# A linear-attention and gated-MLP kernel: ScalarE copies transposed bf16 blocks out of PSUM as fp32 words

## The chip, the cores and the metric

The kernel runs on one core of a Trainium2 chip. A core has TensorE (PE; its weight loads are shown as PEld), VectorE (DVE), ScalarE (ACT), GpSimd (POOL), the SyncE queue (SP) that issues most DMAs, an on-chip memory of 128 partitions (SBUF), and a small one of 8 banks (PSUM) that TensorE writes and VectorE and ScalarE read. The metric is the device time of one execution in microseconds (us). Before the change it is 141.28 us, the median of 3 runs (141.26 to 141.32).

## The reference, cut to what matters

The first stage is a gated linear attention over 4 batches x 8 heads, 768 tokens and 48 columns per head; the second takes its output, all heads side by side (384 columns), through a gated MLP that mixes tokens.

```python
for t in range(S):
    state = alpha[:, :, t, :, None] * state + einsum('bhd,bhe->bhde', k[:, :, t], v[:, :, t])
    y[:, :, t] = einsum('bhd,bhde->bhe', q[:, :, t], state)
x = y.transpose(0, 2, 1, 3).reshape(B, S, H * D)

h = maximum(x @ w_in, 0)
u, v = h[..., :512], h[..., 512:]
v_n = (v - mean(v)) / sqrt(var(v) + 1e-6)
v_s = einsum('ts,bsd->btd', w_spatial, v_n) + b_spatial[None, :, None]
out = (u * v_s) @ w_out
```

## The kernel before, in words

The recurrence is done in chunks of 128 tokens, 6 per batch and 24 in all. Within a chunk the cumulative sum of log(alpha) gives the decays, so that a chunk is a masked product of q and k with v, plus q times the state that the chunks before left. The first eight chunks are done as four **pairs** (function `pair`): 256 tokens are loaded with even and odd tokens next to each other in one partition, so that DMA pieces are longer. The other sixteen chunks are **single** (function `first`).

Products need their contracted dimension on the partitions, so four kinds of blocks are transposed by TensorE, as a matmul of the block with a bf16 identity `ident`. Their bf16 results lie in a PSUM bank and are copied to SBUF by ScalarE or VectorE:

- k and q of a pair (transposes at L502, copies in `ev`, tiles `kT` and `qT`, both named kqT): 512 columns a copy;
- k and q of a single chunk (L710, copies in `ev_qk`, tile `kqT`): 64 columns of 8 blocks, 512 a copy, two copies a chunk;
- the attention output x of a chunk (function `finish_x`; first cast to bf16 as `x_sb`): for a pair's chunk three transposes of 128 columns at L365 and one copy `xe` of 384 columns to `xT`, always by ScalarE; for a single chunk six transposes of 64 columns at L389 and two copies of 192;
- the spatial weight (L831, copies in `weights`, tile `w_spT`): two copies of 384 for each of six row blocks.

All these copies go through the helper `copy` (L196 to L200): `nc.scalar.copy` for ScalarE is L198 in the profile, `tensor_copy` for VectorE and GpSimd L200. For a pair, x comes out of the attention with even tokens first and odd tokens after them. The transposes at L365 keep that order, and the copy `xe` restores the order of tokens: it reads its bank at columns 0, 64, 1, 65 and so on and writes in a row.

The second stage's matmuls (v, u, the spatial mix and the output) are all recorded at L819. Elementwise work around them: `relu` to `v_sb` and `uT` (L204 on ScalarE, L206 on VectorE), normalization (L884 to L916, on VectorE `vn` at L916), the masks of the attention scores (`ptm`, L585 for pairs, L756 for single chunks), the decayed q (`qt`, L481 and L691), and the gate (`gT`, L980).

The order of all this is written out by hand. Every step is an `Op` with a number and the engines that it may run on; the string `PLAN` names for each step its engine and place (`P` TensorE, `D` VectorE, `A` ScalarE, `G` GpSimd, `S` the SyncE queue), and `replay` emits the steps in that order. So each engine's order is fixed, and an engine waits at a step until what it needs is there. PSUM banks are handed out in turn, eight in a ring. Numbers behind a colon in the plan are columns of `junk` matmuls (L188) that TensorE runs ahead of a step early in the kernel.

The pair's transposes and copy, which the change edits:

```python
for ks in range(KS):
    nc.tensor.transpose(xv[:, ks, :], st["x_sb"][:, ks, :], ident)
...
copy(eng, bt[b]["xT"][:, c].rearrange("p k (t two) -> p k t two", two=2),
     st["xv"].rearrange("p k (two t) -> p k t two", two=2))
```

Of the kernel before, what the change touches and what calls it, by code (L numbers as in the profile page):

```python
# [9 lines left out]
FP32 = mybir.dt.float32  # L10
# [114 lines left out]
def kernel(  # L125
# [70 lines left out]
    def copy(eng, out, in_):  # L196
        if eng == "ACT":
            nc.scalar.copy(out=out, in_=in_)  # L198
        else:
            ENG[eng].tensor_copy(out=out, in_=in_)  # L200

    def relu(eng, out, in_):
        if eng == "ACT":
            nc.scalar.activation(out=out, in_=in_, func=AF.Relu)  # L204
        else:
            ENG[eng].tensor_scalar_max(out=out, in0=in_, scalar1=0.0)  # L206
# [140 lines left out]
    def finish_x(i):  # L347

        b, c = divmod(i, NCH)
        t0 = c * C  # L350
        st = T[i]
        P = float(10 * i)

        def xs(eng):
            st["x_sb"] = work.tile([128, KS, 128], BF16, name="x_sb")
            copy(eng, st["x_sb"], st["y"].rearrange("p h d -> p (h d)").rearrange("p (k t) -> p k t", k=KS))

        op(("xs", i), {"ACT": 0.38, "DVE": 0.47}, None, xs, got(("y", i), ("xt", i - WK)), prio=P + 9, use=[st["sl_y"]])

        if i // 2 in PAIRS:  # L360
            def xt(_):
                xv = st["xv"] = st["y"].rearrange("p h d -> p (h d)").bitcast(BF16)[:, 0:KS * 128].rearrange(
                    "p (ks t) -> p ks t", ks=KS)
                for ks in range(KS):
                    nc.tensor.transpose(xv[:, ks, :], st["x_sb"][:, ks, :], ident)  # L365

            op(("xt", i), "PE", 0.2, xt, got(("xs", i)), prio=P + 9, use=[st["sl_y"]], cols=384)

            def xe(eng):
                if b not in bt:  # L370
                    tiles(b)
                copy(eng, bt[b]["xT"][:, c].rearrange("p k (t two) -> p k t two", two=2),
                     st["xv"].rearrange("p k (two t) -> p k t two", two=2))

            made[("xe", i)] = [op(("xe", i), ENGINES["xe"], None, xe,
                                  got(("xt", i)) + [made.get(("all", b - 3))], prio=P + 9, use=[st["sl_y"]])]
            return

        sls = [st["sl_y"], Slot(ring)]
        to = {}  # L380

        def xt(_):
            flat = [st["y"].rearrange("p h d -> p (h d)"), bank([128, DM])]
            for r in range(2):
                to[r] = flat[r].bitcast(BF16)[:, 0:KS * 64].rearrange("p (ks t) -> p ks t", ks=KS)
            for ks in range(KS):
                for r in range(2):
                    rows = slice(64 * r, 64 * r + 64)
                    nc.tensor.transpose(to[r][:, ks, :], st["x_sb"][rows, ks, :], ident[rows, rows])  # L389

        op(("xt", i), "PE", 0.1, xt, got(("xs", i)), prio=P + 9, take=sls[1], use=[st["sl_y"]], cols=192)
        made[("xe", i)] = []
        for r in range(2):
            def xe(eng, r=r):
                if b not in bt:
                    tiles(b)
                copy(eng, bt[b]["xT"][:, c, :, 64 * r:64 * r + 64], to[r])

            made[("xe", i)].append(op(
                ("xe", i, r), {"ACT": 0.25, "DVE": 0.22}, None, xe,  # L400
                got(("xt", i)) + [made.get(("all", b - 3))], prio=P + 9, use=[sls[r]]))
# [12 lines left out]
    def pair(j):  # L414
# [33 lines left out]
        for par in range(2):  # L448
            def cum(_, par=par):
                cm = st[f"cum{par}"] = bank([128, 512])  # L450
                for p2 in range(2):
                    nc.tensor.matmul(  # L452
                        out=cm[:, 0:DM], lhsT=lt_pair if p2 > par else le_pair, rhs=lap[:, p2, :, 0:D],
                        start=(p2 == 0), stop=(p2 == 1))

            op(("cump", j, par), "PE", 0.33 + 0.1, cum, got(("lnp", j), ("c_tri",)), prio=P + 2, take=sl_c[par], cols=768)

            def einv(_, par=par):
                st[f"binv{par}"] = binvp_bufs[(2 * j + par) % 3]
                nc.scalar.activation(  # L460
                    out=st[f"binv{par}"], in_=st[f"cum{par}"][:, 0:DM].rearrange("p (h d) -> p h d", h=H),
                    func=AF.Exp, scale=-1.0)

            op(("einvp", j, par), "ACT", 0.38, einv, got(("cump", j, par), ("ktp", *divmod(2 * j + par - 3, 2))), prio=P + 3,
               use=[sl_c[par]])

            def eexp(_, par=par):
                cv = st[f"cum{par}"][:, 0:DM]
                nc.scalar.activation(out=cv, in_=cv, func=AF.Exp)

            op(("eexpp", j, par), "ACT", 0.38, eexp, got(("einvp", j, par)), prio=P + 3.1, use=[sl_c[par]])

            def ktf(eng, par=par):
                ENG[eng].tensor_mul(
                    out=k_blocks(ktp[:, par])[:, :, :, 0:D],
                    in0=quad(st["kc"][:, :, par, :]), in1=quad(st[f"binv{par}"]))

            op(("ktp", j, par), {"POOL": 0.9, "DVE": 0.6}, None, ktf, got(("einvp", j, par), ("kc", 2 * j), ("c_kt", j % NKP)) + tr_users("k", jo), prio=P + 4)

            def qtf(_, par=par):  # L480
                nc.vector.tensor_mul(  # L481
                    out=qtp[:, par, :, ::-1, 0:D], in0=quad(st["qc"][:, :, par, :]),
                    in1=quad(st[f"cum{par}"][:, 0:DM].rearrange("p (h d) -> p h d", h=H)))

            op(("qtp", j, par), "DVE", 0.47, qtf, got(("eexpp", j, par), ("qc", 2 * j), ("c_qt", j % NKP)) + tr_users("q", jo), prio=P + 4, use=[sl_c[par]])

            def vbf(eng, par=par):
                if "vb" not in st:
                    st["vb"] = pairs.tile([128, 2, H, D], BF16, name="vbp", bufs=3)
                copy(eng, st["vb"][:, par], st["vc"][:, :, par, :])  # L490

            op(("vbp", j, par), {"POOL": 0.47, "ACT": 0.42, "DVE": 0.27}, None, vbf, got(("vc", 2 * j), ("y", 2 * j - 5), ("y", 2 * j - 6)), prio=P + 4.5)

            for nm, bufs in (("k", ktp), ("q", qtp)):
                hold = {}
                sl = Slot(ring)

                def tr(_, par=par, nm=nm, bufs=bufs, hold=hold):
                    pt = bank([128, 512])
                    hold["t"] = pt.bitcast(BF16).rearrange("p (n t) -> p n t", n=8)[:, 0:HP, :]  # L500
                    for hp in range(HP):
                        nc.tensor.transpose(  # L502
                            hold["t"][:, hp, :],
                            k_window(bufs[:, par], hp, 1) if nm == "k"
                            else bufs[:, par, hp].rearrange("p s d -> p (s d)"), ident)

                op(("tr", nm, j, par), "PE", 0.22, tr, got((nm + "tp", j, par), ("c_id",)), prio=P + 5, take=sl, cols=512)

                def ev(eng, par=par, nm=nm, hold=hold):
                    if nm == "k":  # L510
                        if "kT" not in st:
                            st["kT"] = work.tile([128, 2, HP, C], BF16, name="kqT", bufs=4)
                        copy(eng, st["kT"][:, par], hold["t"])
                    else:
                        if "qT" not in st:
                            st["qT"] = work.tile([128, 2, HP, C], BF16, name="kqT", bufs=4).rearrange(
                                "p a h c -> p (a h c)").rearrange("p (h c a t) -> p h c a t", a=2, c=2, h=HP)
                        copy(eng, st["qT"][:, :, :, par, :], hold["t"].rearrange("p h (c t) -> p h c t", c=2))

                op(("ev", nm, j, par), EV, None, ev,  # L520
                   got(("tr", nm, j, par), ("y", 2 * j - 4), ("y", 2 * j - 3), ("sc", j - 2, 0), ("sc", j - 2, 1)),
                   prio=P + 6, use=[sl])
# [102 lines left out]
    def first(i):  # L625
# [91 lines left out]
        for r in range(2):  # L717
            def ev_qk(eng, r=r):
                if "kqT" not in st:
                    st["kqT"] = work.tile([128, 2, HP, C], BF16, name="kqT", bufs=4).rearrange("p a h c -> p (a h) c")  # L720
                copy(eng, st["kqT"][:, :, 64 * r:64 * r + 64], hold[r])

            op(("ev", i, r), ENGINES["ev"], None, ev_qk, got(("trk", i), ("y", i - WK), ("sc", i - WK)),
               prio=P + 6, use=[sls[r]])
# [96 lines left out]
    def weights():  # L821
        for tt in range(NT):
# [12 lines left out]
            op(("wt", tt), "PE", 0.2, emit, got(("cast", "w_sp", tt // 2, tt % 2)), prio=50.0, take=sls, cols=384)  # L835
            for r in range(2):
                def ev(eng, tt=tt, hold=hold, r=r):
                    copy(eng, w_spT[:, tt, :, 64 * r:64 * r + 64], hold[r])

                op(("we", tt, r), {"DVE": 0.3, "ACT": 0.42}, None, ev, got(("wt", tt)), prio=50.0, use=[sls[r]])  # L840

# [318 lines left out]
```

## Time and profile before

| What | Value |
|---|---|
| Median time of 3 runs | 141.28 us (141.26 to 141.32) |
| Span of the profiled execution, first to last instruction | 144.3 us (no other time of this execution is given) |
| Busy: PE, DVE, ACT, POOL | 136.8, 118.7, 106.8, 86.8 us |
| Mean granted TensorE clock | 0.996 |
| Copies of transposed blocks by ScalarE | 24 of kqT, 27 of xT, 5 of w_spT |
| Copies of transposed blocks by VectorE | 24 of kqT, 13 of xT, 7 of w_spT |

A row of a group gives line, engine, operation, the tile written and those read (`out<-in`), partitions x elements and type of each, how many; then busy us, mean ns of one, and the idle time of the engine just before them with what ended it. The mean of one is longer than its share of a queue: instructions that follow each other overlap. The chain of waits goes back from the last instruction, at each step to what released it or to the instruction before it on its engine; its pieces are shown in order of time. "issue" is time in which an engine waited for nothing that the profile shows.

### The profile page before, as it was taken

What the parts mean: (1) busy time and instruction counts of PE and PEld (TensorE: products, weight loads), DVE (VectorE), ACT (ScalarE), POOL (GpSimd) and SP (SyncE); (2) the same over time, 40 slices, a digit from 0 to 9 for tenths busy, and PEclk for the clock granted to TensorE, in tenths of its full rate; (3) what the DMA queues carried; (4) which work ended last, traced back from release to release, by engine and by line L of the source; (5) the groups of instructions that cost most, each with busy time, mean ns of one, the idle gap of its engine ahead of it and who ended that gap; (6) DMA issues with size and microseconds to landing.
All of it is one profiled execution on the core that took longest, in us unless ns stands there. A gap on an engine that the chain in (4) does not pass through costs nothing.

```text
span 144.3 us, 4963 instructions
## 1 busy us (share of the span) xinstructions
PE 136.8 (95%) x1915; PEld 84.2 (58%) x1915; DVE 118.7 (82%) x289; ACT 106.8 (74%) x278; POOL 86.8 (60%) x152
## 2 busy tenths in 40 slices
PE   7799999799799999999999999999999999999990
PEld 3334766656465765676556665665657666555560
DVE  7015798899999969899999999999979897987940
ACT  3473479899895879899997789998797698861031
POOL 6856179892709979981249789511599687002820
PEclk9999999999999999999999999999999999999998
DMA  4999999929899989999899899799999241090055
GB/s 108 321 326 351 282 250 325 344 58 259 181 269 191 300 164 182 205 181 214 169 211 222 175 174 185 152 204 196 212 239 227 66 172 55 0 354 28 5 191 191
DMA packets 89000, 28.64 MB, mean 198 GB/s; under 512 B 83728, under 2 KB 87440, under 8 KB 88976
## 3 DMA queue, kind: packets, MB, share of 16 engines
q1 hardware_dynamic: 88944, 28.32, 79.5%
q8 instruction: 15, 0.25, 0.7%
q14 instruction: 9, 0.07, 0.1%
q0 software_dynamic: 32, 0.00, 0.0%
HBM read 23.60 MB, written 4.72 MB: 196 GB/s over the span
## 4 chain that ended last, share of the span: by engine, by line
PE 78%; DVE 8%; ACT 5%; DMA 3%; issue 3%; SPq 0%; ACTq 0%; DVEq 0%
PE bank L819 47%; PE bank L188 4%; DMA ac<-in_alpha_dram 3%; PE bank L710 3%; PE bank L452 2%; PE bank L502 2%; PE bank L745 2%; PE bank L574 2%; DVE ptm L756 2%; PE bank L773 2%; PE bank L731 2%; PE bank L544 1%; DVE ptm L585 1%; PE bank L657 1%; PE bank L601 1%
## 5 line engine op out<-in xcount | busy, mean ns | idle before, releaser
L819 PE MATMUL bank<-w_spT,vn 128*128 128x384 bf16 x192 | 36.3, 326 | 0.1
L980 POOL TENSOR_TENSOR gT<-vsb,uT 128x384 bf16<-128x384 f32 x28 | 25.7, 927 | 11.7 <-DVE vsb L967 11.2
L335 POOL TENSOR_TENSOR state<-state,bc 128x192 f32<-128x192 f32 x20 | 10.3, 513 | 21.4 <-DVE state L328 6.2
L819 PEld LDWEIGHTS <-vn 128*128 128x128 bf16 x192 | 17.1, 97 | 10.2 <-issue 0.2
L756 DVE TENSOR_TENSOR ptm<-bank,mask 128x512 bf16<-128x512 f32 x32 | 20.8, 682 | 1.0 <-ACT xT L198 1.0
L819 PE MATMUL bank<-xT,w_in 128*128 128x384 bf16 x96 | 19.4, 326 | 0.0
L967 DVE TENSOR_TENSOR vsb<-bank,bsp_bc 128x384 f32<-128x384 f32 x31 | 16.7, 554 | 3.2 <-PE bank L819 2.8
L819 PE MATMUL bank<-w_in,xT 128*128 128x512 bf16 x72 | 18.8, 379 | 0.0
L198 ACT COPY kqT<-bank 128x512 bf16<-128x512 bf16 x24 | 13.6, 590 | 6.9 <-PE bank L502 4.4
L819 PE MATMUL bank<-w_out_sb,gT 128*128 128x384 bf16 (+1 forms) x100 | 18.4, 320 | 0.1
L681 POOL TENSOR_TENSOR kt<-kc,binv 128x384 bf16<-128x384 f32 x13 | 12.0, 927 | 6.6 <-ACT bc L676 2.7
L200 POOL CAST sbd<-state 64x192 bf16<-64x192 f32 x40 | 13.6, 341 | 2.1
L884 DVE BATCH_NORM_STATS2 stats<-v_sb 128x6 f32<-128x512 bf16 x20 | 13.6, 681 | 0.5 <-ACT v_sb L204 0.5
L204 ACT ACTIVATE v_sb<-bank 128x512 bf16<-128x512 f32 x20 | 11.9, 608 | 1.6 <-PE bank L819 1.6
L198 ACT CAST x_sb<-bank 128x384 bf16<-128x384 f32 x21 | 10.2, 493 | 3.5 <-PE bank L773 2.7
L819 PEld LDWEIGHTS <-w_in 128*128 128x128 bf16 x96 | 8.7, 97 | 6.0
L188 PE MATMUL bank<-junk 128*128 128x512 f32 (+2 forms) x16 | 11.1, 838 | 1.1 <-DVE halves_of L264 1.1
L200 DVE COPY kqT<-bank 128x512 bf16<-128x512 bf16 x24 | 9.2, 415 | 3.1 <-PE bank L502 2.3
L819 PEld LDWEIGHTS <-gT 128*128 128x128 bf16 x100 | 8.7, 97 | 5.1 <-POOL gT L980 0.2
L204 ACT ACTIVATE uT<-bank 128x384 bf16<-128x384 f32 x23 | 11.3, 495 | 0.3 <-PE bank L819 0.2
L198 ACT COPY xT<-bank 128x192 bf16<-128x192 bf16 (+1 forms) x27 | 9.1, 378 | 2.4 <-PE bank L365 1.5
L585 DVE TENSOR_TENSOR ptm<-bank,mask 128x512 bf16<-128x512 f32 x16 | 10.2, 682 | 0.7 <-PE bank L574 0.4
(128 smaller groups left out, 285.2 us busy)
## 6 DMA issues: line engine op xcount, KB each, us to landing
ac<-in_alpha_dram SPq DMA_DIRECT2D x16, 192.0 KB, 3.9
kc<-in_k_dram SPq DMA_DIRECT2D x16, 192.0 KB, 4.2
qc<-in_q_dram SPq DMA_DIRECT2D x16, 192.0 KB, 4.0
vc<-in_v_dram SPq DMA_DIRECT2D x16, 192.0 KB, 3.8
raw_w<-in_moe_w_spatial_dram SPq DMA_DIRECT2D x3, 768.0 KB, 4.5
out_dram<-raw_w SPq DMA_DIRECT2D x11, 192.0 KB, 2.0
out_dram<-o_sb SPq DMA_DIRECT2D x9, 192.0 KB, 1.9
ac<-in_alpha_dram SPq DMA_DIRECT2D x4, 384.0 KB, 5.5
```

Of the source, the lines that this page charges most:

```text
L188: nc.tensor.matmul(out=flat[:, 0:cols].rearrange("p (a b) -> p a b", a=4), lhsT=junk, rhs=junk[:, None, 0:n].to_broadcast([128, 4, n]), st ...
L198: nc.scalar.copy(out=out, in_=in_)
L200: ENG[eng].tensor_copy(out=out, in_=in_)
L204: nc.scalar.activation(out=out, in_=in_, func=AF.Relu)
L335: ENG[eng].tensor_tensor(out=st["state"], in0=st["state"], in1=st["bc"][:, :, None].to_broadcast([128, HP, D]), op=ALU.mult)
L585: nc.vector.tensor_tensor(out=st[f"ptm{par}"][:, s], in0=st[f"pt{s}{par}"], in1=mask2[:, par], op=ALU.mult)
L681: ENG[eng].tensor_mul(out=k_blocks(kt3)[:, :, :, 0:D], in0=quad(st["kc"]), in1=st["binv"])
L756: nc.vector.tensor_tensor(out=st["ptm"][:, s], in0=st[f"pt{s}"], in1=mask4, op=ALU.mult)
L819: return lambda ps: nc.tensor.matmul(out=out(ps), lhsT=lhsT(), rhs=rhs(), start=start, stop=stop)
L884: nc.vector.bn_stats(out=stats, in_=d["v_sb"][:, tt, :])
L967: nc.vector.tensor_tensor(out=hold["vs"], in0=ps[:, 0:TH], in1=bsp_bc[:, th, :], op=ALU.add)
L980: ENG[eng].tensor_tensor(out=bt[b]["gT"][:, dsl, cols], in0=hold["vs"], in1=bt[b]["uT"][:, dsl, cols], op=ALU.mult)
```

## The change

On ScalarE, the copies of transposed blocks take both sides as fp32, so that two bf16 elements that lie next to each other are moved as one 4-byte word and an instruction has half the elements. On VectorE they stay as they are. For this the two elements of a word must stay neighbours, which the pair's copy of x, with its order of columns, did not allow. So there the transposes themselves now put tokens in order: the identity is read with its columns in the order 0, 64, 1, 65 and so on, and the copy is a plain one. The bank is written in a row as before. The numbers of instructions, their order on each engine and `PLAN` are the same.

```diff
+    def copy_pairs(eng, out, in_):
+
+        copy(eng, *((out.bitcast(FP32), in_.bitcast(FP32)) if eng == "ACT" else (out, in_)))
+
...
                 for ks in range(KS):
-                    nc.tensor.transpose(xv[:, ks, :], st["x_sb"][:, ks, :], ident)
+                    nc.tensor.transpose(
+                        xv[:, ks, :].rearrange("p (t a) -> p t a", a=2), st["x_sb"][:, ks, :],
+                        ident.rearrange("p (a t) -> p t a", a=2))
...
-                copy(eng, bt[b]["xT"][:, c].rearrange("p k (t two) -> p k t two", two=2),
-                     st["xv"].rearrange("p k (two t) -> p k t two", two=2))
+                copy_pairs(eng, bt[b]["xT"][:, c], st["xv"])
...
-                copy(eng, bt[b]["xT"][:, c, :, 64 * r:64 * r + 64], to[r])
+                copy_pairs(eng, bt[b]["xT"][:, c, :, 64 * r:64 * r + 64], to[r])
...
-                        copy(eng, st["kT"][:, par], hold["t"])
+                        copy_pairs(eng, st["kT"][:, par], hold["t"])
...
-                        copy(eng, st["qT"][:, :, :, par, :], hold["t"].rearrange("p h (c t) -> p h c t", c=2))
+                        copy_pairs(eng, st["qT"][:, :, :, par, :], hold["t"].rearrange("p h (c t) -> p h c t", c=2))
...
-                copy(eng, st["kqT"][:, :, 64 * r:64 * r + 64], hold[r])
+                copy_pairs(eng, st["kqT"][:, :, 64 * r:64 * r + 64], hold[r])
...
-                    copy(eng, w_spT[:, tt, :, 64 * r:64 * r + 64], hold[r])
+                    copy_pairs(eng, w_spT[:, tt, :, 64 * r:64 * r + 64], hold[r])
```

## The prediction

> **What bounds the kernel now.** I read the page first, then TensorE's waits, its busy time by stretches, and the chain of waits in order of time.
>
> ```profile
> span 144.3 us, 4963 instructions
> ...
> PE 136.8 (95%) x1915; PEld 84.2 (58%) x1915; DVE 118.7 (82%) x289; ACT 106.8 (74%) x278; POOL 86.8 (60%) x152
> ...
> PE 78%; DVE 8%; ACT 5%; DMA 3%; issue 3%; SPq 0%; ACTq 0%; DVEq 0%
> ```
>
> TensorE (PE) is busy for 95% of the span and holds 78% of the chain that ended last; ScalarE (ACT), which the change relieves, holds 5%. Next, what TensorE's matmuls ever waited for, in full (who waited, for whom, us in total, times, longest):
>
> ```profile
> PE bank L188 <- DVE halves_of L264: 1.1, 1, 1.1
> PE bank L452 <- ACT la L443: 0.9, 1, 0.9
> PE bank L502 <- DVE kqT L200: 0.8, 1, 0.8
> PE bank L574 <- issue: 0.8, 1, 0.8
> PE bank L544 <- issue: 0.3, 1, 0.3
> ```
>
> These come to 3.9 us. One of them ends with ScalarE, and that is a logarithm of loaded data, no copy that changes. So a faster ScalarE has no wait of its own to remove; it can only help through VectorE (DVE). The stretches (PE, PEld, DVE, ACT, POOL busy) show how near VectorE is:
>
> ```profile
> 42.00:48.00 6.00, 6.00 (x148) 3.88 (x146) 5.73 (x15) 4.30 (x13) 4.48 (x7) 1.00 1.03 240
> 66.00:72.00 6.00, 6.00 (x87) 3.52 (x84) 5.93 (x17) 5.97 (x22) 0.81 (x2) 1.00 0.99 192
> 72.00:78.00 6.00, 5.87 (x83) 3.71 (x81) 5.75 (x14) 5.46 (x17) 3.88 (x6) 1.00 1.06 210
> ```
>
> Late in the kernel TensorE is never idle in a stretch, or by 0.13 us of 6. Now the chain, piece by piece (start us, us, what), where L365 are the transposes that change:
>
> ```profile
> 21.89 0.17 PE bank L365 x3
> ...
> 22.47 0.29 issue
> ...
> 23.21 0.27 PE bank L365 x3
> ...
> 27.65 0.76 issue
> ...
> 29.46 1.89 DVE ptm L585 x3
> ...
> 33.48 0.34 PE bank L365 x6
> 33.82 0.50 PE bank L819 x3
> ...
> 34.34 1.02 DVE uT L206 x2
> 35.37 1.84 DVE vn L916 x4
> 37.21 0.33 DVE kqT L200
> 37.54 1.25 DVE w_row L200 x2
> ...
> 38.84 0.35 PE bank L831 x12
> ...
> 49.53 0.34 PE bank L365 x6
> ...
> 66.91 1.12 ACT xT L198 x4
> ...
> 72.95 0.55 DVE qt L691
> ...
> 73.54 2.60 PE bank L819 x15
> ```
>
> The reader is to see three parts: up to 39 us TensorE and VectorE pass the path to and fro; from 39 to 61 us, and again from 73.5 us, the pieces are almost all TensorE's; between them VectorE and ScalarE are named, while TensorE beside them is full. Eighteen of the 24 changed transposes (3 + 3 + 6 + 6) lie on this path.
>
> **The change part by part.** *The ScalarE copies.* Same instructions and same order, half the elements. The groups (line, engine, names, shapes, count | busy us, mean ns of one | idle before):
>
> ```profile
> L198 ACT COPY kqT<-bank 128x512 bf16<-128x512 bf16 x24 | 13.6, 590 | 6.9 <-PE bank L502 4.4 <-PE bank L710 2.1 <-DVE w_row L200 0.4
> ...
> L198 ACT COPY xT<-bank 128x192 bf16<-128x192 bf16 x19 | 5.3, 335 | 0.9 <-PE bank L389 0.9
> L198 ACT COPY raw_w<-bank 128x384 f32<-128x384 f32 x9 | 4.4, 484 | 0.8 <-PE bank L819 0.7 <-issue 0.2
> ...
> L198 ACT COPY xT<-bank 128x384 bf16<-128x384 bf16 x8 | 3.7, 480 | 1.5 <-PE bank L365 1.5
> ...
> L198 ACT COPY w_spT<-bank 128x384 bf16<-128x384 bf16 x5 | 2.3, 480 | 0.3 <-PE bank L831 0.2
> ...
> L198 ACT COPY raw_w<-bank 128x192 f32<-128x192 f32 x1 | 0.3, 325 | 0.0
> ```
>
> A copy costs by elements, not bytes: 384 fp32 take 484 ns and 384 bf16 480; 192 take 325 and 335. The slope is (480 - 335)/192 = 0.76 ns per element below 384 and (590 - 480)/128 = 0.86 above; I use 0.81. Then 256 words take 335 + 64 x 0.81 = 387 ns, 192 words 330, 96 words 335 - 96 x 0.81 = 257. Saved: 24 x 203 = 4.9 us (kqT), 8 x 150 = 1.2 (xT of the pairs), 5 x 150 = 0.75 (w_spT), 19 x 78 = 1.5 (xT of the single chunks); 8.3 us in all, off 106.8. On the path I count none of it. Before 39 us VectorE or TensorE releases each piece. At 66.91 us the chain does name four changed copies, but VectorE, which hands on to TensorE at 72.95, is itself busy 5.93 of the 6 us there, so its own queue is as late. After that TensorE has no wait left to lose. The cover is thus VectorE's queue between 61 and 73 us; if it were gone, the copies would be worth what the second rival says.
>
> *Tokens in order, in the transpose.* Earlier the ScalarE copy of xT read the bank 64 elements apart to restore the order; it cost nothing (480 ns, like the w_spT copy that reads in a row), so ending that saves nothing beside the halving. Now the identity, TensorE's moving operand, is read 64 elements (128 bytes) to and fro for each column. No row of this kernel shows a moving operand read so. Bounds:
>
> ```profile
> 10.17 4.25 PE bank L188 x6
> 14.43 1.12 PE bank L502 x20
> ```
>
> Low end: nothing. A transpose of 128 columns takes 1.12/20 = 56 ns in a row, and the changed ones as much (0.34/6 = 57); a gain is excluded, because the column count, which sets this time, stays. High end: the slowest moving operand in the trace, 512 columns of fp32 at 4.25/6 = 708 ns, is 177 ns per 128 columns, so +121 ns each. Between them I go by the only reads 64 elements apart that the trace has, ScalarE's xT: they run at the 0.81 ns per element worked out above, and nothing shows such reads faster. 128 of these are 104 ns, so +47 ns each over 57. TensorE at 56/128 = 0.44 ns per column would need nearly twice that rate.
>
> [...]
>
> *Where +47 ns lands.* First group, 21.89: 3 x 47 = 0.14, taken up by the 0.29 us of "issue" at 22.47, in which TensorE waits for nothing shown by the profile. Second, 23.21: +0.14, which I carry on, since the "issue" at 27.65 ends before VectorE's masks (29.46) and follows TensorE's own progress; low end 0, if that wait hides it, high end 0.36. The third six:
>
> ```profile
> 28.76 0.34 PE L365 MATMUL bank<-ident,x_sb 128*128 128x128 bf16 x3
> ...
> 29.26 0.33 PE L365 MATMUL bank<-ident,x_sb 128*128 128x128 bf16 x3
> ...
> 31.14 0.81 PE L601 MATMUL bank<-vbp,ptm 64*128 64x48 bf16 x32
> ```
>
> They cost nothing: L601 behind them waits for VectorE's masks until 31.35 (29.46 + 1.89). The six at 33.48 delay the three matmuls at 33.82 and with them VectorE's uT at 34.34. VectorE was ready there at 34.26:
>
> ```profile
> 34.08 0.18 DVE L885 BATCH_NORM_AGGREGATE mvs<-stats 128x2 f32<-128x6 f32 x1
> ```
>
> So it is 6 x 47 = 0.28, less 0.08, or +0.20. VectorE is then occupied to 38.8 us (34.34 through 37.54 + 1.25) and TensorE waits there, so this passes on in full. The six at 49.53 stand in a full TensorE: +0.28. Sum: 0.14 + 0.20 + 0.28 = +0.62 us.
>
> DVE's copies, POOL, the DMAs and their issue order stay. ScalarE frees its PSUM banks and inputs up to 0.2 us sooner, so some loads may be issued sooner; TensorE's list shows no wait for a DMA, so I count nothing.
>
> **Sum.** The profiled execution spans 144.3 us, 3.0 us over the median 141.28 (no other time for it is given), and I carry the difference over as it is: 144.3 + 0.6 = 144.9 profiled, 141.28 + 0.62 = 141.9 timed (+0.4%). A measurement of this kernel can tell about 0.2%, or 0.28 us, from no change.
>
> **Rivals.** *First, the strided identity is free.* For it: the same order was free to ScalarE. Against it: TensorE reads nearly twice as fast. Then nothing on the path changes: 141.2, with 0 to 0.1 us gained in small pieces.
>
> *Second, faster: the copies are on the path after all, and the identity is free.* For it: the chain of waits runs through ScalarE at 66.91. Four copies of 78 ns less are 0.31 us; one more is on it at 83.10:
>
> ```profile
> 83.10 0.33 ACT xT L198
> ```
>
> That makes 0.39, 140.9 us. It decides only if VectorE's qt at 72.95 is really released by ScalarE and not by its own queue. Against it: VectorE's 5.93 of 6 us, and TensorE's 0.13 us of idle time in the next stretch, which is all that an earlier qt could win at once.
>
> *Third, a transpose at the high end.* With +121 ns: first group 0.36 - 0.29 = 0.07, second 0.36, then 0.73 - 0.08 = 0.65 and 0.73: +1.8, 143.1 us. For it: nothing but that the bound is open. Against it: no bf16 row of a warm TensorE comes near 177 ns per 128 columns.
>
> **How the numbers follow.** Forecast 0.47, first rival 0.25, second 0.18, third 0.10. The forecast's own range, with +25 to +80 ns a transpose (the parts above scale to +0.3 and +1.1), is 141.6 to 142.4. Faster by over 0.2%: the second rival and a tail of the first, 0.19. Within 0.2%: most of the first rival and the forecast's lowest edge, 0.27. Slower: the rest, 0.54. The range runs from the second rival, 140.9, to 142.6; left out are most of the third rival and the edges of the second, some 0.17.
>
> **What would show it.** Right: kqT copies near 387 ns with 256 fp32 elements, xT near 330 and 257, w_spT near 330, ScalarE near 98.5 us busy; the group of 24 transposes (line 369 then) at about 100 ns apart in the chain instead of 57; VectorE's uT later by 0.3 us; from 49.5 us on everything shifted by 0.6 us with unchanged gaps. Wrong: transposes still 57 ns apart (then 141.2), or VectorE's qt before the L819 matmuls of 73.54 earlier against the uT of 34.34 than it is now (then the copies were on the path). A fetch or "issue" wait of other length at 22 or 27 us would also upset the sum, by a few tenths.

## The result, and the profile after

The changed kernel takes 142.55 us (median of 4 runs) against 141.28 us before. Every kernel here that ran more than once has some executions that are 1.6 to 3.6% longer than its fastest on the same chip; they are left out of the ratios and of the ranges below, but not of this median, which counts one run of 146.01 us. The other three took 142.05, 142.51 and 142.59 us, and the ratio is 1.0076, 95% interval [1.0059, 1.0092]: slower, by 1.1 us. Measured again (run f1 below) the ratio was 1.0075 [1.0039, 1.0111].

In the profile of before that the prediction shows, TensorE's first matmuls took 1.7 times as long as in the profile of after (the six L188 matmuls at 10.17 us 4.25 us; after and in run e0 2.57), and all else came some 3 us later. The kernel after is therefore compared here with a second profile of before, run e0, whose execution took 141.9 us. The page of each, after first (lines of code behind the new helper are 4 or 5 higher: L365 became L369, L819 became L824):

```profile
span 140.3 us, 4963 instructions
...
PE 134.6 (96%) x1915; PEld 84.0 (60%) x1915; DVE 117.9 (84%) x289; ACT 99.4 (71%) x278; POOL 86.8 (62%) x152
...
PE 81%; DMA 6%; ACT 5%; DVE 4%; issue 1%; SPq 0%; ACTq 0%; DVEq 0%
```

And before, run e0:

```profile
span 140.1 us, 4949 instructions
...
PE 132.6 (95%) x1901; PEld 83.0 (59%) x1915; DVE 118.4 (84%) x289; ACT 106.5 (76%) x278; POOL 86.6 (62%) x152
```

And run e2 of the experiments, which has the change's identity and the copies of before:

```profile
PE 134.1 (95%) x1901; PEld 84.0 (60%) x1915; DVE 118.0 (84%) x289; ACT 106.7 (76%) x278; POOL 87.1 (62%) x152
```

ScalarE has 7.1 us less to do, TensorE 2.0 us more, and TensorE was the bound. (The 2.0 is not exact: e0's profile has 1901 matmul records of 1915. Run e2, with 1901 too, has 1.5 us more than e0.) Where each comes from is in the groups of after (line, engine, names, shapes, count | busy us, mean ns of one | idle before):

```profile
L198 ACT COPY kqT<-bank 128x256 f32<-128x256 f32 x24 | 8.5, 377 | 5.4 <-PE bank L715 2.7 <-PE bank L507 2.7
...
L369 PE MATMUL bank<-ident,x_sb 128*128 128x128 bf16 x24 | 3.9, 285 | 0.0
L198 ACT COPY xT<-bank 128x96 f32<-128x96 f32 x19 | 3.8, 255 | 1.7 <-PE bank L394 1.5
```

and in before, run e0, the transposes' group:

```profile
L365 PE MATMUL bank<-ident,x_sb 128*128 128x128 bf16 x24 | 2.3, 220 | 0.1
```

The copy of kqT went from about 590 ns to 377, the pairs' transposes from 220 ns to 285: 65 ns more each, 24 times, 1.56 us of TensorE's time. How much of that is on the path is read from the chain of waits in order of time (start us, us, what). I set it against run e1 of the experiments, which differs from after only in the pairs' x: their transposes read the identity in a row and their copy is the one of before, all other copies are by words. After:

```profile
17.74 0.28 PE bank L619 x4
...
28.98 0.49 PE bank L824 x3
29.47 0.73 PE bank L369 x6
...
35.10 1.57 PE bank L824 x9
...
45.09 0.73 PE bank L369 x6
...
137.02 0.36 ACTq L1160
```

Run e1:

```profile
17.89 0.29 PE bank L618 x4
...
28.93 0.49 PE bank L823 x3
29.42 0.34 PE bank L369 x6
29.75 0.50 PE bank L823 x3
30.28 1.02 DVE uT L210 x2
...
34.65 1.57 PE bank L823 x9
...
44.64 0.34 PE bank L369 x6
...
136.18 0.36 ACTq L1159
```

Six transposes in a row take 0.73 us instead of 0.34: 122 ns each instead of 57. Between the rows that both chains name:

| Stretch | e1 | after | more | transposes in it |
|---|---|---|---|---|
| 17.89 / 17.74 to 28.93 / 28.98 | 11.04 | 11.24 | 0.20 | 12, worth 0.78 if none were hidden |
| to 34.65 / 35.10 | 5.72 | 6.12 | 0.40 | 6, worth 0.39 |
| to 136.18 / 137.02 | 101.53 | 101.92 | 0.39 | 6, worth 0.39 |

That is 0.99 us more from 17.9 us on; after came to that point 0.15 us sooner, so it ends 0.84 us later, and the times of these two executions, 142.05 and 141.21, differ by the same 0.84. Three quarters of what the first twelve transposes cost are hidden; each of the other two groups of six shows in full.

The ratios of after and of e1 to before (1.0076 and 0.9977) are 1.0% or 1.4 us apart (1.1 to 1.7 by the two intervals), 0.6 us more than these two profiles. The profiled execution of after was the fastest of its runs (142.05, the next 142.51). So other executions lose more than this profile shows, and where the other 0.6 us lie is open. One candidate is the order of two casts at 33 us, described with e1 below: with GpSimd's first the path was 0.52 us longer. In the profile of after VectorE's came first (33.29 us against 33.94), in e2's by 0.02 us (33.64 against 33.66), and after the change VectorE comes there 0.45 us later than in e1, so nearer to being second. This is not shown: no execution of the changed kernel near 142.5 was profiled.

### The profile page after: what moved, and what is told of

The parts are those of the page before. It is cut to its first block, busy times and chain, and to the rows that moved or that the text cites. A ratio compares the mean times of both kernels' runs of the same rounds, so it can differ in the third digit from the quotient of the medians.

```text
span 140.3 us, 4963 instructions
## 1 busy us (share of the span) xinstructions
PE 134.6 (96%) x1915; PEld 84.0 (60%) x1915; DVE 117.9 (84%) x289; ACT 99.4 (71%) x278; POOL 86.8 (62%) x152
## 3 DMA queue, kind: packets, MB, share of 16 engines
q1 hardware_dynamic: 88944, 28.32, 81.8%
## 4 chain that ended last, share of the span: by engine, by line
PE 81%; DMA 6%; ACT 5%; DVE 4%; issue 1%; SPq 0%; ACTq 0%; DVEq 0%
PE bank L824 49%; PE bank L188 3%; PE bank L715 3%; DMA ac<-in_alpha_dram 3%; PE bank L507 3%; DMA qc<-in_q_dram 3%; PE bank L750 3%; PE bank L369 2%; PE bank L457 2%; PE bank L778 2%; PE bank L579 2%; PE bank L736 2%; PE bank L662 2%; PE bank L394 1%; PE bank L772 1%; PE bank L549 1%
## 5 line engine op out<-in xcount | busy, mean ns | idle before, releaser
L824 PE MATMUL bank<-w_spT,vn 128*128 128x384 bf16 x192 | 36.3, 326 | 0.1
L824 PEld LDWEIGHTS <-vn 128*128 128x128 bf16 x192 | 17.1, 97 | 10.2 <-issue 0.2
L339 POOL TENSOR_TENSOR state<-state,bc 128x192 f32<-128x192 f32 x20 | 10.3, 514 | 17.8 <-DVE state L332 6.5
L824 PE MATMUL bank<-xT,w_in 128*128 128x384 bf16 x96 | 19.4, 326 | 0.0
L824 PE MATMUL bank<-w_in,xT 128*128 128x512 bf16 x72 | 18.7, 379 | 0.0
L824 PE MATMUL bank<-w_out_sb,gT 128*128 128x384 bf16 (+1 forms) x100 | 18.4, 320 | 0.1
L824 PEld LDWEIGHTS <-w_in 128*128 128x128 bf16 x96 | 8.7, 97 | 6.1
L198 ACT COPY kqT<-bank 128x256 f32<-128x256 f32 x24 | 8.5, 377 | 5.4 <-PE bank L715 2.7
L824 PEld LDWEIGHTS <-gT 128*128 128x128 bf16 x100 | 8.7, 97 | 5.1 <-POOL gT L985 0.3
L188 PE MATMUL bank<-junk 128*128 128x512 f32 (+2 forms) x16 | 9.3, 720 | 1.1 <-DVE halves_of L268 1.1
L674 ACT ACTIVATE binv<-bank 128x384 bf16<-128x384 f32 x16 | 7.8, 490 | 3.4 <-PE bank L665 2.3
```

The costliest lines, as they stand in the source:

```text
L188: nc.tensor.matmul(out=flat[:, 0:cols].rearrange("p (a b) -> p a b", a=4), lhsT=junk, rhs=junk[:, None, 0:n].to_broadcast([128, 4, n]), st ...
L339: ENG[eng].tensor_tensor(out=st["state"], in0=st["state"], in1=st["bc"][:, :, None].to_broadcast([128, HP, D]), op=ALU.mult)
L824: return lambda ps: nc.tensor.matmul(out=out(ps), lhsT=lhsT(), rhs=rhs(), start=start, stop=stop)
```

## The experiments

Ratios are to the kernel before, run on the same chip in turn, with 95% intervals.

**e0: the kernel before again**, for its profile.

> The kernel before once more, unchanged, for a profile to set beside the changed one. Both theories: the time is 141.2 to 141.4 us; the groups of three and six L365 transposes stand 56 to 57 ns apart as before.

One run, 141.9 us, span 140.1: 0.5 us over what was expected, and within the range of before on that chip (141.33 to 142.08). The transposes stand 57 ns apart, as expected. It is the profile of before used here.

**e1: words alone.** The change without its edit of the pairs' x:

```diff
-                    nc.tensor.transpose(
-                        xv[:, ks, :].rearrange("p (t a) -> p t a", a=2), st["x_sb"][:, ks, :],
-                        ident.rearrange("p (a t) -> p t a", a=2))
+                    nc.tensor.transpose(xv[:, ks, :], st["x_sb"][:, ks, :], ident)
...
-                copy_pairs(eng, bt[b]["xT"][:, c], st["xv"])
+                copy(eng, bt[b]["xT"][:, c].rearrange("p k (t two) -> p k t two", two=2),
+                     st["xv"].rearrange("p k (two t) -> p k t two", two=2))
```

> ScalarE's copies as fp32 words everywhere but in the pairs' x, which keeps the plain identity and the reordering bf16 copy. Theory (the copies lie off the path, the strided identity alone costs): 141.1 to 141.4 us, ScalarE about 7 us less busy, the transposes 57 ns apart. Rival 1 (the copies are on the path and hide part of the identity's cost): 140.9 us or less. Rival 2 (shorter copies cost time themselves, by loads that start sooner and collide): 141.8 us or more.

Measured: 0.9977 [0.9962, 0.9992], runs 141.00 to 141.60. The copies were not worth nothing. The timelines (start us, us, engine, line, operation, names, shapes, count, in brackets the idle time before and who ended it) show where. Before, run e0:

```profile
22.33 1.11 ACT L198 COPY kqT<-bank 128x512 bf16<-128x512 bf16 x2
23.28 0.91 ACT L443 ACTIVATE la<-ac 128x768 bf16<-128x768 f32 x1
24.02 0.54 ACT L198 CAST x_sb<-bank 128x384 bf16<-128x384 f32 x1
24.38 0.26 ACT L550 ACTIVATE bc<-bank 128x8 f32<-128x8 f32 x1
...
24.74 0.36 DVE L330 TENSOR_TENSOR state<-bank,state 128x192 f32<-128x192 f32 x1
25.01 2.48 DVE L585 TENSOR_TENSOR ptm<-bank,mask 128x512 bf16<-128x512 f32 x4
...
33.00 1.58 DVE L200 CAST w_row<-raw_w 128x768 bf16<-128x768 f32 x2
...
32.87 0.82 POOL L200 CAST w_row<-raw_w 128x768 bf16<-128x768 f32 x1 [2.55 <-DMA raw_w<-in_moe_w_spatial_dram]
```

Words alone, run e1:

```profile
22.36 0.68 ACT L198 COPY kqT<-bank 128x256 f32<-128x256 f32 x2
22.88 0.91 ACT L447 ACTIVATE la<-ac 128x768 bf16<-128x768 f32 x1
23.82 0.48 ACT L198 CAST x_sb<-bank 128x384 bf16<-128x384 f32 x1
24.20 0.18 ACT L554 ACTIVATE bc<-bank 128x8 f32<-128x8 f32 x1
...
24.59 0.35 DVE L334 TENSOR_TENSOR state<-bank,state 128x192 f32<-128x192 f32 x1
24.85 2.48 DVE L589 TENSOR_TENSOR ptm<-bank,mask 128x512 bf16<-128x512 f32 x4
...
32.84 1.02 DVE L200 CAST w_row<-raw_w 128x768 bf16<-128x768 f32 x2
...
33.00 1.54 POOL L200 CAST w_row<-raw_w 128x768 bf16<-128x768 f32 x1 [2.86 <-DMA raw_w<-in_moe_w_spatial_dram]
```

Two kqT copies at 22.3 us end 0.4 us sooner, and what stands behind them in ScalarE's queue follows: x_sb ends at 24.30 instead of 24.56, `bc` (the factors for the state) at 24.38 instead of 24.64. VectorE's `state`, just ahead of the masks in its queue, waits for ScalarE there (by the trace's semaphores, which do not say whether for x_sb or `bc`): in e0 it starts 0.10 us after `bc` ends, in e1 right behind VectorE's own work, 24.59 for 24.74. The masks, for which TensorE waits next, come 0.16 us sooner (24.85 for 25.01). That is the words' gain on the path. In this pair of profiles 0.52 us of the path come on top at 33 us: before, GpSimd's cast started first and VectorE's two took 1.58 us; in e1 VectorE's started first, took 1.02 us, and GpSimd's took 1.54 instead of 0.82. VectorE came there 0.16 us sooner, but the load that GpSimd's cast waits for also came 0.13 us later, so part of this is chance. From 35 us on there is nothing to gain: e0 goes from 35.33 to its last piece at 136.88, 101.55 us, and e1 needs 101.53.

**e2: the strided identity alone.** The change with all copies left in bf16 (`copy` in place of every `copy_pairs`).

> The strided identity alone, all copies in bf16 as before; the pairs' xT copy is a plain one of 384. Theory: as the changed kernel, 142.0 to 142.6 us, transposes about 121 ns apart. Rival 1 (the copies win some of the loss back): 142.7 us or more. Rival 2 (the shorter copies cost the time): 141.2 to 141.5 us.

Measured: 1.0097 [1.0073, 1.0121], runs 142.42 to 143.19. That is 1.4 us of loss by the identity alone, at the border between the theory and its first rival. With e1, 0.97 - 0.23 = 0.74%, which is the change's own 0.76%: within the intervals the two edits add up, and the loss is the identity's.

**e3: words, and the identity reordered once.** GpSimd writes a second identity whose columns lie in the order 0, 64, 1, 65; the transposes then read it in a row:

```diff
+    ident_ta = consts.tile([128, 128], BF16, name="ident_ta")
...
+                nc.gpsimd.tensor_copy(
+                    out=ident_ta.rearrange("p (t a) -> p t a", a=2), in_=ident.rearrange("p (a t) -> p t a", a=2))
...
-                    nc.tensor.transpose(
-                        xv[:, ks, :].rearrange("p (t a) -> p t a", a=2), st["x_sb"][:, ks, :],
-                        ident.rearrange("p (a t) -> p t a", a=2))
+                    nc.tensor.transpose(xv[:, ks, :], st["x_sb"][:, ks, :], ident_ta)
```

To make room, two pads (32 bytes behind `eps_tile`, 224 behind a `vsb` buffer) were taken out; the tiles between them so lie 224 bytes higher.

> The changed kernel with a second identity whose columns are stored in the order 0, 64, 1, 65 and so on, written once by GpSimd, so that TensorE reads it in a row; all copies as words. Theory: 141.1 to 141.4 us, transposes 56 to 57 ns apart, no gain over the kernel before although ScalarE is 8 us less busy. Rival 1: 140.9 us or less. Rival 2: 141.8 us or more.

Measured: 1.0422 [1.0373, 1.0471], far from what any theory had expected. The page (span; the load queue's packets, MB, share of 16 engines' span) and the chain of e3:

```profile
span 146.8 us, 4949 instructions
...
q1 hardware_dynamic: 88944, 28.32, 89.3%
...
51.42 0.35 PE bank L373 x6
```

The transposes themselves are as fast as before the change, six in 0.35 us, so something else costs 6 us: the packets of the load queue take 131 us (89.3% of 146.8) instead of 115 after the change (81.8% of 140.3), for the same bytes. That pointed to the moved tiles. Not all of the 6 us need be the loads': in this profile TensorE's first matmuls are slow too (the six L188 3.91 us), and beside f1, a profile of the changed kernel with the same trait (4.43 us, span 144.5), e3 is 2.3 us longer.

**e3b: the same with the tiles moved by 256 bytes** (192 behind the `vsb` buffer): the `eps_tile` pad stays, the other is cut from 224 to 160 bytes.

> As the run with the stored order, but the padding of eps_tile stays and the last vsb buffer's padding shrinks by 64 bytes, so that every later tile moves by whole 64 bytes (256, or 192 behind vsb), and not by 224. If the addresses made that run slow: 141.0 to 141.4 us, DMA packets' share of the engines' span back near 82%, transposes 56 to 57 ns apart. If the second identity or its copy on GpSimd made it slow: 146 us or more again. Theory of the copies: about 0.2% under the kernel before, as with the words alone.

Measured: 1.0048 [0.9902, 1.0194], unclear, as the interval is wide; the best two took 141.53 and 141.62 us. The 6 us are gone, with the same instructions: the profile spans 139.8 us, and the packets take 115 us again (81.9% of it). f2 below measures it again.

**e5: the kernel before, its tiles moved by 32 bytes**, nothing else:

```diff
-    eps_tile = consts.tile([128, 9], FP32, name="eps_tile")[:, 0:1]
+    eps_tile = consts.tile([128, 1], FP32, name="eps_tile")
```

> The kernel before with eps_tile without its padding, which moves all later tiles by 32 bytes and changes nothing else. If addresses off the 64-byte grid slow the DMAs: 144 us or more, with a DMA share over 85%. If not: 141.2 to 141.8 us.

Measured: 1.0527 [1.0367, 1.0687], 148.4 us at best, against 141.5 and 141.9 of before on that chip. Addresses alone do this. How much of the 7 us is the loads' own is less sure: the six L188 matmuls take 4.76 us in e5's profile, and beside the prediction's profile of before, with 4.25, its span is 2.8 us longer (147.1 for 144.3). Whether the moved tiles also bring about the slow first matmuls these runs do not show. What the loads show is below, with f4.

**e4: four orders of reading the identity**, one for each pair of chunks; the bank is written in a row as before (the lines for that are left out here), and all else is the changed kernel's:

```diff
+                    n = i // 2
+                    order = (ident.rearrange("p (a t e) -> p t a e", a=2, e=2),
+                             ident.rearrange("p (a t e) -> p t a e", a=2, e=8),
+                             ident.rearrange("p (t e) -> p e t", e=2),
+                             ident.rearrange("p (t e) -> p e t", e=8))[n]
...
```

> The changed kernel with another reading order of the identity for each pair of chunks, so the tokens of the first eight chunks come out in a wrong order; the work is the same. Pair 0: runs of two columns (4 bytes), 64 columns apart; pair 1: runs of eight (16 bytes), 64 apart; pair 2: every second column, then the others; pair 3: every eighth column, then the next, so that each read is 16 bytes on. [...] Rival (any order but in a row costs): all four at about 121. Rival (only far jumps cost): pair 3 at 57, pair 0 between.

The chain of e4 names three of the four orders:

```profile
21.91 0.20 PE bank L377 x3
...
32.41 0.34 PE bank L377 x6
...
47.64 1.37 PE bank L377 x6
```

and TensorE's timeline the one of the second pair (in this view three in a row count 0.34 us when they read in order, as at 24.61 us in e0 and 24.46 in e1):

```profile
27.68 0.34 PE L377 MATMUL bank<-ident,x_sb 128*128 128x128 bf16 x3
```

| How 128 columns (2 bytes each) are read | ns a transpose |
|---|---|
| in a row (e1) | 57 |
| runs of 8 columns (16 bytes), 128 bytes to and fro (pair 1) | as in a row |
| every second column, then the others (pair 2) | 0.34/6 = 57 |
| runs of 2 columns, 128 bytes to and fro (pair 0) | 0.20/3 = 67 |
| single columns, 128 bytes to and fro (the change) | 0.73/6 = 122 |
| every eighth column, so 16 bytes on each time (pair 3) | 1.37/6 = 228 |

The leap of 128 bytes as such cost nothing: runs of eight columns leap as far as the change does and took 57 ns. With that leap the time rose as the runs got shorter, to 67 ns for two columns and 122 for one. Steps of two columns cost nothing either (57), steps of eight took 228. Runs of two columns and steps of eight cost more than the author's estimate (67 ns for 56 to 60, 228 for about 121); both rivals are excluded by pairs 1 and 2 at 57 and pair 3 at 228. Single columns to and fro between two places 128 bytes apart cost less (122) than going on by 16 bytes each time (228); why, these orders do not show.

**e6: e3b with two of VectorE's kqT copies given to ScalarE**, which now has time: steps D350 and D340 of `PLAN` become A350 and A340.

> The aligned kernel with stored order, and two copies of q of the fourth pair (512 columns each) moved from VectorE to ScalarE at their places in the plan, in the stretch from 28 to 34 us where VectorE holds the path. Theory (time freed on ScalarE counts only where it takes work off the engine that holds the path): 140.5 to 140.9 us, 0.3 us or more below the aligned kernel with stored order. Rival (ScalarE is itself the path there): no faster than that kernel.

Measured: 1.0047 [0.9877, 1.0216], unclear, best 141.46. The chain says that it gains early and, in that execution, lost it again:

```profile
33.88 0.35 PE bank L581 x16
...
79.67 4.78 DMA kc<-in_k_dram
84.61 0.92 POOL kt L688
```

The same sixteen matmuls start at 34.51 in f2, the run of e3b below; then TensorE waited for GpSimd's `kt` behind a late load.

**f1, f2, f3: after, e3b and e6 again**, all three on one chip.

> The changed kernel again, beside the next two on one chip. My account now (slower transposes cost 1.2 to 1.4 us, the words gain 0.3 us) expects 1.0 us over the kernel before, ratio 1.007. If the first measurement was a chance of its chip, the ratio is within 0.998 to 1.003.

> The words everywhere, the reordered identity stored in order, tiles moved by whole multiples of 64 bytes; again, since the chip of its first measurement was disturbed. My account: the transposes cost what they did before and the words gain what they gain alone, ratio 0.9977 (0.3 us faster than before, 1.3 us faster than the change). Rival, that the words gain only with the plain identity or that the extra GpSimd copy costs what they gain: 1.000.

> As the one before it, with two of VectorE's kqT copies given to ScalarE, which has the time for them now. My account, from its first profile (0.4 us ahead at 34 us and at 80 us): ratio 0.995, 0.7 us faster than the kernel before. Rival, that what is ahead at 80 us is lost to later waits for loads, as in its first profile: 0.998 or above.

Measured: after 1.0075 [1.0039, 1.0111]; e3b 0.9989 [0.994, 1.0038]; e6 0.9958 [0.9911, 1.0006]. Against the changed kernel both gain: the intervals do not overlap, if barely for e3b, and the changed kernel's runs (f1) are 142.50 to 143.03, those of f2 140.94 to 142.93 with a median of 141.3, those of f3 140.81 to 142.70 with a median of 140.9. Against the kernel before neither interval excludes no change; five of f3's six runs (140.81 to 141.04) lie below all 22 of before (141.28 and more), the sixth (142.70) does not. In f2's chain the transposes cost what they did before the change:

```profile
29.62 0.33 PE bank L373 x6
...
34.51 0.35 PE bank L581 x16
```

So the words can be had without the slower transposes; that this beats the kernel before (by 0.1% as it stands, by 0.4% with the two copies moved) is likely, not shown.

**f4: the kernel before, its tiles moved by 64 bytes** (`eps_tile` padded to 25 words; the tiles behind the `vsb` buffer stay where they were).

> The kernel before with a pad of 64 bytes more behind a small constant, so that all tiles after it lie 64 bytes higher (96 bytes higher than in the run moved by 32 bytes less), and nothing else. If it is the distance from a grid of 64 bytes that slows the loads: ratio 1.000 within 0.003, and a load queue share of about 82%. If any move off the present addresses costs, as off a grid of 128 bytes or more: 1.04 or above, and a share near 88%.

Measured: 1.022 [1.013, 1.0309], between the two expectations. The queue's packets (count, MB, share of 16 engines' span) and the issues of the pairs' loads (queue, count, KB each, median us to landing) tell more. Before, run e0:

```profile
q1 hardware_dynamic: 88944, 28.32, 81.4%
...
kc<-in_k_dram SPq DMA_DIRECT2D x4, 384.0 KB, 5.6
```

Moved by 32 bytes, run e5:

```profile
q1 hardware_dynamic: 88944, 28.32, 87.9%
...
kc<-in_k_dram SPq DMA_DIRECT2D x4, 384.0 KB, 7.0
```

Moved by 64 bytes, run f4:

```profile
q1 hardware_dynamic: 88944, 28.32, 82.4%
...
kc<-in_k_dram SPq DMA_DIRECT2D x4, 384.0 KB, 6.9
```

The pairs' loads, early in the kernel, take 6.9 or 7.0 us instead of 5.6. Times the spans (140.1, 147.1, 146.6), the packets took 114, 129 and 121 us. Moved by 256 bytes (f2) it is 115 us, 82.7% of 139.5. This does not come with slow first matmuls: the prediction's profile of before has them too, and 5.9 us for a pairs' load and 115 us for the packets (79.5% of 144.3). Beside it f4, with 3.85 us for the six L188, is 2.3 us longer. In the profiles of e3, e5 and f4 the granted clock is lower as well (0.986, 0.977 and 0.988, in the others 0.996 and more). What part of this that takes is not shown; runs of the same kernels at 0.997 to 1.0 took 146.68, 148.41 and 147.01 us, where the profiled ones took 148.54, 148.89 and 148.40.

The single packets of the traces narrow down what kind of grid it would be; that it is a grid at all is inferred, as the traces show no addresses. The pairs' loads are pieces of 384 bytes, of which 99% took 22 ns in e0 and in f2, but only 27 to 28% in e3, e5 and f4; their mean rose from 22.3 to 28 ns. The single chunks' loads are pieces of 192 bytes: 97% took 15 ns in e0 and f2, 69% in e3, 76% in e5, and 95% in f4. So the move by 64 bytes slowed the long pieces and hardly the short ones. A grid of 64 bytes is excluded: both lengths are multiples of 64, so f4 would have slowed neither. A grid of 128 or 256 bytes fits: pieces of 192 bytes one behind the other begin at every multiple of 64 on it, and a move by 64 leaves that set as it is, while pieces of 384 begin at multiples of 128 only, if the tiles did before, and the moves by 32, 64 and 224 all take them off.

## Why the prediction was right, and where it was off

It forecast 141.9 us, +0.4%, in a range of 140.9 to 142.6, and slower as the likeliest sign. Measured: +0.76%, or 1.07 us where 0.62 was forecast. The sign and the mechanism (a slower read of the identity, paid by TensorE: 122 ns a transpose for 57) are right; the size is short by 0.45 us.

- **A copy costs by elements.** Right: 377 ns for kqT (387 forecast) and 255 for xT of single chunks (257). ScalarE's busy time is 99.4 us (98.5 forecast).
- **The copies are worth nothing on the path.** Wrong by little: 0.23% [0.08, 0.38], about 0.3 us, by e1. The argument was that no matmul ever waited for a changed copy. It missed that a copy delays what stands behind it in ScalarE's queue: at 22.3 us the two kqT copies stand ahead of x_sb and `bc`, for which VectorE's `state` at 24.7 us, ahead of the masks, waits. Nor does VectorE or TensorE release each piece before 39 us: e0's chain has two changed copies there (xT at 19.05 and 20.26 us), which the prediction's profile, with its slower start, did not show. The second rival had this mechanism, at 66.91 us; there, late in the kernel, e1 gains nothing, as the cover of VectorE's queue had it.
- **The strided identity costs 47 ns a transpose.** Here lies the error: the term was mis-sized, and 65 ns were measured (122 ns for 104). ScalarE's read 64 elements apart, the nearest row, was no measure of TensorE's. That the bounds of 0 and 121 held for this order was luck: the upper one came from the slow first matmuls of that profile (4.25 us for six), and by e0's row (2.57/6 = 428 ns, or 107 per 128 columns) it would have been +50, below what was measured. e4 has an order outside either (+171). So the leap of 128 bytes does not set the price by itself: in e4 runs of eight columns with the same leap took 57 ns, runs of two 67.
- **The first twelve are mostly hidden (forecast +0.14).** Near it, +0.20 of 0.78 by the table of stretches, but in part by luck, as it falls elsewhere. The first six, of which +0.14 was to pass on, delayed the masks by 0.07 us (after, 0.15 us ahead of e1 at 17.8 us, has them 0.08 ahead, 24.77 for 24.85). The last six of the twelve, forecast to cost nothing, cost the other 0.13. TensorE itself hid most of them in its wait for VectorE's masks, which e1's list of waits has and after's has no more:

```profile
PE bank L605 <- DVE ptm L589: 0.3, 1, 0.3
```

But in after's chain the L457 matmuls behind these transposes (25.64 us) hold up ScalarE's binvp (26.00) and VectorE's qt (27.29), which the L507 matmuls at 28.36 need; the forecast looked at TensorE's own wait alone. The "issue" waits at 22 and 27 us of the prediction's profile are not in the chain of after. What hides most of the first six is in e1's chain: there TensorE waits until 20.71 us for ScalarE's xT (20.29 us), and in after TensorE's own matmuls fill that time.
- **The six at 33.48, +0.20.** Too low: +0.40. At 65 ns they are 0.39, and VectorE's 0.08 us, taken off in the forecast, was not there: in e1 the three matmuls ahead of uT end at 30.25 and uT starts at 30.28, so TensorE was already last. After, VectorE waits for TensorE:

```profile
30.73 1.02 DVE L210 TENSOR_SCALAR uT<-bank 128x384 bf16<-128x384 f32 x2 [0.48 <-PE bank L824]
```

- **The six at 49.53, +0.28.** Right place, in full and with unchanged gaps behind; +0.39 at 65 ns.
- **The sum.** In the places of its three terms 0.20 + 0.40 + 0.39 = 0.99 us were measured instead of 0.62, and the words take 0.3 off, which it had at 0. That alone would be 0.7, so that two errors of the forecast partly cancel; 1.07 was measured. The remainder of 0.4 us, which the profile of after does not contain, stays open (the order of the two casts at 33 us is a candidate, not shown).
- **The other rivals.** The first (a free identity) is excluded by e2, and with it the second, which needed one; that copies are on the path was right in it. The third, 121 ns more a transpose, overstated it by nearly two.

## What to carry to other kernels

A change that relieves one engine and moves a little work to the engine that bounds the kernel is priced on the second: 65 ns times 24 outweighed 7 us of ScalarE. Put an order into stored data once (with a reordered identity six transposes took 0.33 us in f2) rather than into how a matmul reads it each time (0.73 with the change). If an operand must be read with leaps, try longer runs at each place: with leaps of 128 bytes, runs of 16 bytes took here what a row takes (57 ns a transpose), runs of 4 bytes 67, single columns 122. Before calling a shorter instruction worthless because nobody waits for it, look at what stands behind it in its queue and who waits for that.

## What was not expected of the hardware

- **Addresses of tiles.** With tiles moved by 32, 64 or 224 bytes the kernels ran 5%, 2% and, with the stored identity, 4% longer (beside profiles with slow first matmuls too 2.8, 2.3 and 2.3 us); by 256 bytes nothing measurable. In those three cases the pieces of 384 bytes took 28 ns on average instead of 22.3. These packets fit a grid of 256 bytes, but one of 128 as well, and a move by 128 bytes was not tried.
- **VectorE's and GpSimd's casts at the same time.** In both profiles the engine that started later took longer, by nearly all that the other still had to run: 0.56 us of 0.69 in e0 (VectorE, 1.58 us for 1.02), 0.72 of 0.86 in e1 (GpSimd, 1.54 for 0.82). In e1 this went on over both of VectorE's casts. Why, the traces do not show.
- **Reading a matmul's moving operand** cost up to four times as much for the same columns: 57 to 228 ns for 128 columns, by order alone (e1, e4).
